# Attention and soft mixture of experts in one kernel: block sums as one product over four heads, the last values moved ahead of the last routing, shorter rings and three more weight buffers

## The chip, the cores and the metric

The kernel runs on one NeuronCore of a Trainium2 chip. The metric is the device time of one execution in microseconds (us), lower is better. The engines are TensorE (PE; its weight loads are listed apart as PEld), VectorE (DVE), ScalarE (ACT), GpSimd (POOL) and SyncE (SP), which issues the transfers between the chip's main memory and the on-chip buffers. Matrix products are written to PSUM banks, and DVE or ACT copies them out.

## The reference

Attention over 4 batches, 8 heads, 768 positions and 64 columns: each query sees the keys less than 16 positions away and 24 block keys. A block key is the largest value of each column over 32 positions; a block value is the mean over the same 32 positions. A soft mixture of 8 experts with 4 slots each follows on the 3072 x 512 result. All is float32.

```python
k_sum = k.reshape(B, H, nb, block, D).max(axis=3)
v_sum = v.reshape(B, H, nb, block, D).mean(axis=3)
scores_l = scale * np.matmul(q, k.transpose(0, 1, 3, 2))          # kept where |i - j| < 16
scores_s = scale * np.einsum('bhsd,bhnd->bhsn', q, k_sum) + np.log(block)
a = softmax(np.concatenate([scores_l_m, scores_s], axis=-1))
x = np.matmul(a, np.concatenate([v, v_sum], axis=2))              # to 3072 x 512
...
logits = x @ phi                                                  # 32 slots
d, c = softmax(logits, axis=0), softmax(logits, axis=1)
slot_input = d.T @ x
slot_out[e] = np.maximum(slot_input[e] @ w1[e], 0.0) @ w2[e]      # 8 experts, hidden 1024
return c @ slot_out
```

## The kernel before

**Steps.** The attention is cut into 24 steps (`NSTEP`): 8 half-batches `hb` of four heads, three steps each (`TPS`), and a step has 256 positions. The engines' work is written out by hand as three steps in flight. In loop turn `i` (L543) stand the scores of step `i` (L227, PE), their masked maxima (`soft_max`, L246, DVE) and exponentials; for the first head pair the exponential takes the maximum as a bias (L256, four ACT instructions), for the second POOL subtracts first (L262) and one ACT instruction follows (L258). The same turn transposes the weights of step `i-1` (`trans`, L268, PE; copied out by `evac`, L273, ACT) and multiplies those of step `i-2` with the values (`values`, L284, PE), which DVE divides by the sums (`norm`, L302 to L305). Each engine works through its own instructions in the order written; every wait is for another engine or a transfer.

**Block values.** `v_sum(hb)` (L313) forms the 24 block sums of four heads. A 0/1 matrix out of the constants picks the blocks; for each of 6 tiles of 128 positions, 2 halves `c` and 4 heads `g` there is one product of 32 x 64 outputs (L320), 48 in all. Half `c` has its own PSUM bank, and head `g` writes partitions 32g to 32g+31. Then four ACT copies (L331) and four DVE additions (L333) bring the 24 rows of each head to partitions 96 to 119 of `vsst`, and from there POOL copies them into the value tiles (`put_v`, L340), two copies a step. A table (`PLAN`, L41) says after which step each `V` begins (steps 0, 2, 5, 8, 11, 14, 17, 20): its products are issued at the end of that turn, its copies at the start of the next, ahead of that turn's `soft_max` (`held`, `flush`, L552).

**Routing.** The same table places the routing of the finished rows `x`: `X` transposes 128 rows (L351, copied by ACT, L354), `L` multiplies with `phi` (L364) and keeps a running maximum and its exponentials, `T` and `D` transpose these and add up `slot_input` (L396, L399, L407, L422). After the last step three more turns (24 to 26) hold the rest of the attention mixed with `X18` to `X23`, `L4`, `L5`, `T4` and `D4`; `T5`, `D5` and a few small products (`lanes`, `slots`) close it.

**Experts.** 64 weight pieces of 512 KB are read in order, the first 32 by the product `hps` (L647), the other 32 by `so` (L680), whose result is combined with the routing (`op`, L717) and written out. `LOADS` (L65) says how many pieces SP issues after each step. A piece goes to one of 39 places (`room`, L127): 17 buffers of its own (`NWA`), and tiles of the attention from the step on at which they are free.

**Rings.** The value tiles form a ring of 8 (`NV`), each loaded by two transfers (L160, L161) eight steps ahead of its use; the rows `x` a ring of 6 (`NX`); queries and keys have two buffers each, loaded at every third step (L151, L155).

Of the kernel before, what the change touches and what calls it, by code (L numbers as in the profile page):

```python
# [9 lines left out]
F32 = mybir.dt.float32  # L10
F32R = mybir.dt.float32r
AF = mybir.ActivationFunctionType
ALU = mybir.AluOpType
# [5 lines left out]
NB = S // 32  # L19
HB = 2 * B  # L20
TPS = 3
NSTEP = HB * TPS
NTT = 2 * TPS
# [14 lines left out]
NV, NQR, NX, NWA = 8, 2, 6, 17  # L38
# [21 lines left out]
    24: "X18 X19 | L4",  # L60
    25: "T4 ; X20 X21 | D4",
    26: "X22 X23 | L5",
}

LOADS = [0, 1, 1, 1, 1, 1, 1, 1, 1, 1, 1, 1, 1, 1, 1, 1, 1, 1, 1, 1, 5, 1, 1, 7, 1, 1, 2]  # L65
# [10 lines left out]
def attention_soft_moe(  # L76
# [13 lines left out]
    nc = tc.nc  # L90
# [24 lines left out]
    qs = [const.tile([128, TPS, 2, 256], F32, name=f"q{n}") for n in range(NQR)]  # L115
# [7 lines left out]
    qflat = [q.rearrange("p t r k -> p (t r k)")[:, 0:1024] for q in qs]  # L123
# [3 lines left out]
    room = [(t, 0) for t in was] + [(vflat[0], 18), (vflat[1], 19), (vflat[2], 20)]  # L127
    room += [(t, 20) for t in kflat[0] + [qflat[0]]] + [(vflat[3], 21), (vflat[4], 22), (vflat[5], 23)]
    room += [(t, 23) for t in kflat[1] + [qflat[1]] + xflat[0:2]] + [(vflat[6], 24), (vflat[7], 25)]
    room += [(t, 26) for t in xflat[2:4]] + [(t, 27) for t in xflat[4:]]  # L130
# [121 lines left out]
    def soft_exp(i, r):  # L252
        p, m = p_[i, r]
        if r == 0:
            for u in range(4):
                nc.scalar.activation(out=p[:, u, :], in_=p[:, u, :], func=AF.Exp, scale=-1.0, bias=m[:, u : u + 1])  # L256
        else:
            nc.scalar.activation(out=p, in_=p, func=AF.Exp)  # L258
# [12 lines left out]
    def evac(i, r):  # L271
        ptr = wk.tile([128, 4, 128], F32, name="ptr", bufs=4)
        nc.scalar.copy(out=ptr, in_=ptr_[i, r])  # L273
        ptr_[i, r] = ptr
# [38 lines left out]
    def v_sum(hb):  # L313
        pv = [post_bank(), post_bank()]
        for t in range(NTT):
            v = vs[(hb * TPS + t // 2) % NV]
            for c in range(2):
                for g in range(4):
                    o = C_IND + 22 - 2 * (2 * t + c)
                    nc.tensor.matmul(  # L320
                        pv[c][32 * g : 32 * g + 32, 0:64],
                        lhsT=cs[64 * c : 64 * c + 64, o : o + 32],
                        rhs=v[64 * c : 64 * c + 64, c, t % 2, g, 0:64],
                        start=(t == 0),
                        stop=(t == NTT - 1),
                        tile_position=(64 * c, 32 * g),
                    )
        yield
        st = vsst[96 : 96 + NB, hb % 2]
        for g in range(4):  # L330
            nc.scalar.copy(out=st[:, g, 0:64], in_=pv[0][32 * g : 32 * g + NB, 0:64])  # L331
        for g in range(4):
            nc.vector.tensor_tensor(  # L333
                out=st[:, g, 0:64], in0=pv[1][32 * g : 32 * g + NB, 0:64], in1=st[:, g, 0:64], op=ALU.add
            )
# [11 lines left out]
    def route_x(t):  # L347
        pv = post_bank()
        for c in range(4):
            x = xh[t // 2][:, t % 2, 128 * c : 128 * c + 128]  # L350
            nc.tensor.transpose(pv[:, 128 * c : 128 * c + 128], x, ident)  # L351
        yield
        xt = wk.tile([128, 4, 128], F32, name="xt", bufs=6)
        nc.scalar.copy(out=xt.rearrange("p c t -> p (c t)"), in_=pv)  # L354
        ps["xt", t] = xt


    def route_l(q):
# [17 lines left out]
        dt = wk.tile([128, 128], F32, name="dt", bufs=2)  # L376
# [17 lines left out]
    def route_t(q):  # L394
        pv = post_bank()
        nc.tensor.transpose(pv[:, 0:128], ps["dt", q], ident)  # L396
        yield
        dsb = wk.tile([128, 128], F32, name="dsb", bufs=2)
        nc.vector.tensor_copy(out=dsb, in_=pv[:, 0:128])  # L399
        ps["d", q] = dsb  # L400
# [96 lines left out]
    def flush(gs):  # L497
        for g in gs:
            while advance(g):
                pass  # L500
# [42 lines left out]
    for i in range(NSTEP + 3):  # L543
# [4 lines left out]
        if i < NSTEP:  # L548
            scores(i)
        if i == NSTEP + 1:  # L550
            tail.append(1)
        flush(held)  # L552
        if 0 <= a < NSTEP:
# [4 lines left out]
        if i < NSTEP:  # L558
            soft_max(i, 0)
            soft_exp(i, 0)  # L560
            soft_max(i, 1)
            soft_sub(i, 1)
# [5 lines left out]
        if 0 <= a < NSTEP:  # L568
            trans(a, 0)
            trans(a, 1)  # L570
            evac(a, 0)
            evac(a, 1)
        for group in front.split(";"):
            flush(begin(group))
        if i < NSTEP:
            soft_exp(i, 1)
        if 0 <= b < NSTEP:
            values(b)
            norm(b)
# [8 lines left out]
    flush(held)  # L588
    now[0] = NSTEP + 3
    gt = begin("T5")  # L590
    R = lanes()
# [10 lines left out]
    while len(wt) < NPRE:  # L602
        load_piece()
# [217 lines left out]
```

## Time and profile before

| | us |
|---|---|
| median of 3 runs | 222.17 |
| the 3 runs | 218.8, 222.17, 223.51 |
| the profiled execution, its own time | 219.1 |
| span of the profiled execution, first to last instruction | 217.3 |
| attention: first scores to the last product of `L5` | 9.0 to 154.7 |
| experts: first product of `hps` to the end of the span | 160.3 to 217.3 |

The profile is one execution of the program. Times in it count from its first instruction. "Busy" is the time in which an engine had an instruction running; the chain is the work that ended last, followed back from the end to what released each piece; "issue" is idle time of an engine for which the profile shows no releaser. A product of two float32 matrices stands in it as two MATMUL records, each with a LDWEIGHTS record; a transpose stands as one of each.

### The profile page before, as it was taken

The numbers are of one execution on the slowest core, as the hardware profiler recorded it, in microseconds if no ns is written. First come the engines' busy times: TensorE is split into PE (matmuls) and PEld (weight loads), VectorE is DVE, ScalarE is ACT, GpSimd is POOL, SyncE is SP. The second block draws the span as 40 slices with busy tenths as digits, with TensorE's granted clock in tenths as the row PEclk, the third lists the DMA queues.
The fourth block names the chain that finished last, engine by engine and source line by source line (L and its number), as shares of the span: only waits on it lengthen the run. The fifth ranks groups of instructions, "written<-read, shape, count | busy, mean of one in ns | idle before, by whom it ended". The sixth has DMA issues, their size and how long they took to land.

```text
span 217.3 us, 8616 instructions
## 1 busy us (share of the span) xinstructions
PE 178.3 (82%) x3473; PEld 132.1 (61%) x3473; DVE 128.4 (59%) x670; ACT 107.4 (49%) x277; POOL 76.6 (35%) x140
## 2 busy tenths in 40 slices
PE   7686986789879497986949998987789999999760
PEld 5464865677757485875739785874444555644450
DVE  1659597676869458686843866835345755033470
ACT  2057586757747465775545677773400222023360
POOL 8517659336528245642714554440010000000000
PEclk9888899999999889999975999999966999999997
DMA  6999999999967977894892539769998999998767
GB/s 221 329 376 290 376 270 250 369 242 284 358 191 246 336 200 217 306 263 135 269 296 76 149 119 310 272 210 360 420 323 269 391 418 417 419 415 354 305 276 303
DMA packets 19384, 63.19 MB, mean 291 GB/s; under 512 B 2320, under 2 KB 2320, under 8 KB 19344
## 3 DMA queue, kind: packets, MB, share of 16 engines
q1 hardware_dynamic: 19200, 62.28, 84.5%
q8 instruction: 27, 0.44, 0.9%
q10 hardware_dynamic: 144, 0.36, 0.5%
q14 instruction: 13, 0.11, 0.1%
HBM read 56.34 MB, written 6.29 MB: 288 GB/s over the span
## 4 chain that ended last, share of the span: by engine, by line
PE 53%; DVE 13%; ACT 10%; issue 8%; POOL 7%; DMA 6%; SPq 0%; POOLq 0%; ACTq 0%
PE hps L647 8%; PE so L680 7%; PE s L227 7%; PE pt L268 6%; PE o L284 6%; DVE p L246 5%; DMA kk<-kx 3%; PE op L717 3%; POOL p L262 3%; PE pp L351 3%; PE pp L407 3%; DMA q<-qx 3%; ACT xt L354 3%; ACT ptr L273 2%; PE pp L320 2%
## 5 line engine op out<-in xcount | busy, mean ns | idle before, releaser
L256 ACT ACTIVATE p<-p,m 128x128 f32<-128x128 f32 x96 | 30.7, 390 | 34.7 <-DVE m L246 34.7
L246 DVE CUSTOM_DVE_ANT_0 p<-s,cs 128x128 f32<-128x128 f32 x192 | 42.5, 286 | 8.8 <-PE s L227 8.3
L262 POOL TENSOR_TENSOR p<-m,p 128x512 f32<-128x512 f32 x24 | 24.9, 1038 | 61.4 <-DVE m L246 60.5
L227 PE MATMUL s<-kk,q 64*64 64x128 f32 x768 | 30.1, 282 | 12.1 <-issue 7.1
L227 PEld LDWEIGHTS s<-kk,q 64*64 64x64 f32 x768 | 23.1, 136 | 19.0 <-issue 13.6
L284 PE MATMUL o<-v,ptr 120*64 120x65 f32 (+1 forms) x768 | 29.8, 232 | 4.8 <-issue 4.8
L284 PEld LDWEIGHTS o<-v,ptr 120*64 120x64 f32 (+1 forms) x768 | 26.0, 144 | 9.5 <-issue 9.2
L340 POOL COPY v<-vsst 24x520 f32<-24x520 f32 x48 | 29.5, 615 | 5.8 <-DVE vsst L333 3.1
L268 PE MATMUL pt<-ident,p 128*128 128x128 f32 x192 | 29.9, 300 | 1.1 <-ACT p L258 0.9
L273 ACT COPY ptr<-pt 128x512 f32<-128x512 f32 x48 | 25.5, 577 | 3.1 <-PE pt L268 3.0
L268 PEld LDWEIGHTS pt<-ident,p 128*128 128x128 f32 x192 | 22.6, 151 | 6.7 <-issue 3.2
L180 DVE TENSOR_REDUCE ks<-kk 128x8 f32<-128x256 f32 x48 | 17.1, 412 | 6.7 <-DMA kk<-kx 6.6
L258 ACT ACTIVATE p<-p 128x512 f32<-128x512 f32 x24 | 15.3, 639 | 9.0 <-POOL p L262 9.0
L305 DVE TENSOR_TENSOR x<-o,z 128x256 f32<-128x256 f32 x48 | 18.1, 418 | 0.8
L246 DVE DVE_READ_ACCUMULATOR2_ANT m<- 128x1 f32 x192 | 15.9, 83 | 0.0
L302 DVE TENSOR_SCALAR z<-o 128x8 f32<-128x8 f32 x24 | 3.9, 164 | 19.2 <-PE o L284 18.9
L351 PE MATMUL pp<-ident,x 128*128 128x128 f32 x88 | 13.1, 296 | 0.0
L354 ACT COPY xt<-pp 128x512 f32<-128x512 f32 x22 | 12.2, 598 | 1.2 <-PE pp L351 1.2
L320 PE MATMUL pp<-v,cs 64*32 64x64 f32 x768 | 10.5, 235 | 2.3 <-issue 1.7
L351 PEld LDWEIGHTS pp<-ident,x 128*128 128x128 f32 x88 | 11.6, 156 | 0.0
L333 DVE TENSOR_TENSOR vsst<-pp,vsst 24x64 f32<-24x64 f32 x32 | 7.2, 224 | 7.3 <-ACT vsst L331 6.5
L647 PE MATMUL hps<-wa,W1ST 128*32 128x256 f32 x136 | 10.9, 468 | 0.5 <-DVE rz L479 0.5
(137 smaller groups left out, 217.0 us busy)
## 6 DMA issues: line engine op xcount, KB each, us to landing
wa<-w SPq DMA_DIRECT2D x34, 512.0 KB, 8.2
v<-w SPq DMA_DIRECT2D x12, 512.0 KB, 7.0
kk<-kx SPq DMA_DIRECT2D x7, 800.0 KB, 7.2
q<-qx SPq DMA_DIRECT2D x7, 768.0 KB, 9.7
v<-va SPq DMA_DIRECT2D x24, 195.0 KB, 6.6
v<-vb SPq DMA_DIRECT2D x24, 195.0 KB, 6.3
kk<-w SPq DMA_DIRECT2D x9, 512.0 KB, 7.4
x<-w SPq DMA_DIRECT2D x6, 512.0 KB, 7.7
```

Of the source, the lines that this page charges most:

```text
L227: nc.tensor.matmul(s[r][64 * c : 64 * c + 64, u, :].rearrange("p (a k) -> p a k", a=2), lhsT=qs[hb % NQR][64 * r : 64 * r + 64, tp, pr, o ...
L246: nc.vector.tensor_tensor_reduce(out=p[:, u, :], in0=s[:, u, :], in1=maskv[:, mk, :], scale=-0.125, scalar=-NEG, op0=ALU.add, op1=ALU.min, ...
L256: nc.scalar.activation(out=p[:, u, :], in_=p[:, u, :], func=AF.Exp, scale=-1.0, bias=m[:, u : u + 1])
L262: nc.gpsimd.tensor_tensor(out=p, in0=m.unsqueeze(2).broadcast_to([128, 4, 128]), in1=p, op=ALU.subtract)
L268: nc.tensor.transpose(pt[:, u, :], p[:, u, :], ident)
L273: nc.scalar.copy(out=ptr, in_=ptr_[i, r])
L284: nc.tensor.matmul(o[64 * c : 64 * c + 64, r, u, :], lhsT=ptr[0:K, u, 64 * c : 64 * c + 64], rhs=v[0:K, c, tt, 2 * pr + r, :], start=True, ...
L305: nc.vector.tensor_tensor(out=x[:, r], in0=o[:, r, :, 0:64].rearrange("p (t q) d -> p t q d", t=2), in1=z[:, r].rearrange("p (t q) -> p t ...
L340: eng.tensor_copy(out=vs[i % NV][n0 : n0 + NB, c].rearrange("n t h c -> n t (h c)"), in_=src.broadcast_to([NB, 2, 260]))
L351: nc.tensor.transpose(pv[:, 128 * c : 128 * c + 128], x, ident)
L354: nc.scalar.copy(out=xt.rearrange("p c t -> p (c t)"), in_=pv)
L647: nc.tensor.matmul(hps[32 * j : 32 * j + 32, :], lhsT=W1ST[:, c, 32 * e : 32 * e + 32], rhs=t[:, j, :], start=(k == 0), stop=(k == 31), ti ...
```

## The change

**Block sums.** `v_sum` takes all four heads of a tile and half in one product of 32 x 256 outputs: 12 products in place of 48. The four groups of 32 partitions now hold the sums of the tiles t with t % 4 = g, so partial sums. One ACT copy and one DVE addition over 128 x 256 (tile `vp`) join the two banks, one product with the constant `stk` (a matrix that adds rows 32 apart) folds the four groups, and one ACT copy brings 24 x 256 to `vsst`. The fold is issued after the next step's scores, and the last copy after that step's first four exponentials: `held` is advanced once after `scores`, and flushed after `soft_exp(i, 0)`.

PE, around the second block sum (V1, after step 2); first the kernel before, where `o` are the values' outputs, `pp` a bank of block sums and `s` scores:

```order
L284 MATMUL o<-v_93,ptr 64x65 x16
L320 MATMUL pp<-v_96,cs 32x64 x16
L320 MATMUL pp<-v_97,cs 32x64 x16
L320 MATMUL pp<-v_98,cs 32x64 x16
L227 MATMUL s_477<-kk_90,q_92 64x128 x2
```

and the changed kernel at the same place:

```order
L283 MATMUL o<-v_92,ptr 64x65 x16
L319 MATMUL pp<-v_95,cs 32x256 x4
L319 MATMUL pp<-v_96,cs 32x256 x4
L319 MATMUL pp<-v_97,cs 32x256 x4
L226 MATMUL s_400<-kk_90,q 64x128 x2
```

Each row of 16 products has become a row of 4 that are four times as wide. The fold stands behind the eight score rows that follow; PE in the changed kernel from the last of them on:

```order
L226 MATMUL s_401<-kk_90,q 64x128 x2
L332 MATMUL pp<-vp,cs 128x256
L267 MATMUL pt<-ident,p 128x128 x8
L283 MATMUL o<-v_93,ptr 64x65 x16
L226 MATMUL s_487<-kk_90,q 64x128 x2
```

The fold (L332) is ahead of the transposes, which had followed the scores directly. On ACT, the same place before, from the second exponential of step 2 on:

```order
L258 ACTIVATE p<-p 128x512
L331 COPY vsst<-pp 24x64 x4
L256 ACTIVATE p<-p,m 128x128 x4
L273 COPY ptr<-pt 128x512 x2
```

and in the changed kernel (here from the last block sum, V7, on):

```order
L257 ACTIVATE p<-p 128x512
L329 COPY vp<-pp 128x256
L255 ACTIVATE p<-p,m 128x128 x4
L334 COPY vsst<-pp 24x4x64
L272 COPY ptr<-pt 128x512 x2
```

Four small copies ahead of the exponentials became one wide copy ahead of them and one behind them.

**The end of the attention.** The turns 24 to 26 are written out apart from the loop. In the last step both head pairs take the exponential with the bias on ACT, and POOL subtracts nothing; one of step 22's two copies of transposed weights goes to DVE. PE, from the last two steps' weights to the end of `L5`, before (`tl` and `pp` are banks, `x_105`, `x_106` the last rows):

```order
L268 MATMUL pt<-ident,p 128x128 x8
L351 MATMUL pp<-ident,x_104 128x128 x8
L284 MATMUL o<-v_99,ptr 64x65 x16
L364 MATMUL pp<-xt,cs 32x128 x16
L396 MATMUL tl<-ident,dt 128x128
L351 MATMUL pp<-ident,x_105 128x128 x4
L351 MATMUL tl<-ident,x_105 128x128 x4
L284 MATMUL o<-v_100,ptr 64x65 x16
L407 MATMUL pp<-x_103,dsb 32x512 x2
L407 MATMUL pp<-x_104,dsb 32x512 x2
```

and in the changed kernel (`x_99`, `x_100` are the last rows there):

```order
L283 MATMUL o<-v_92,ptr 64x65 x16
L267 MATMUL pt<-ident,p 128x128 x4
L283 MATMUL o<-v_93,ptr 64x65 x16
L267 MATMUL pt<-ident,p 128x128 x4
L352 MATMUL pp<-ident,x_103 128x128 x8
L283 MATMUL o<-v_94,ptr 64x65 x16
L365 MATMUL pp<-xt,cs 32x128 x16
L352 MATMUL tl<-ident,x_99 128x128 x4
L352 MATMUL pp<-ident,x_99 128x128 x4
L352 MATMUL tl<-ident,x_100 128x128 x4
```

The last values (the third L283 row) stand ahead of `L4` (L365) and of the last four transposed row tiles; `T4` and `D4` now follow `L5`.

**Rings and buffers.** `NV` goes from 8 to 7, `NX` from 6 to 5, `NWA` from 17 to 20; the ring of transposed rows `xt` from 6 to 4, `dt` and `dsb` from 2 to 1. The two query buffers lie side by side, so that a third weight piece fits into them. With that `room` has 41 places, and `LOADS` is drawn up anew.

```diff
-NV, NQR, NX, NWA = 8, 2, 6, 17
+NV, NQR, NX, NWA = 7, 2, 5, 20
...
-    24: "X18 X19 | L4",
-    25: "T4 ; X20 X21 | D4",
-    26: "X22 X23 | L5",
...
     def v_sum(hb):
         pv = [post_bank(), post_bank()]
         for t in range(NTT):
             v = vs[(hb * TPS + t // 2) % NV]
+            g = t % 4
             for c in range(2):
-                for g in range(4):
...
+                nc.tensor.matmul(
+                    pv[c][32 * g : 32 * g + 32, 0:256],
+                    lhsT=cs[64 * c : 64 * c + 64, o : o + 32],
+                    rhs=v[64 * c : 64 * c + 64, c, t % 2, :, 0:64],
+                    start=(t < 4),
+                    stop=(t + 4 >= NTT),
+                    tile_position=(64 * c, 32 * g),
+                )
+        yield
+        vp = wk.tile([128, 256], F32, name="vp", bufs=1)
+        nc.scalar.copy(out=vp, in_=pv[0][:, 0:256])
+        nc.vector.tensor_tensor(out=vp, in0=pv[1][:, 0:256], in1=vp, op=ALU.add)
+        sp = post_bank()
+        nc.tensor.matmul(sp[:, 0:256], lhsT=stk, rhs=vp, start=True, stop=True)
+        yield
+        nc.scalar.copy(
+            out=vsst[96 : 96 + NB, hb % 2, :, 0:64], in_=sp[96 : 96 + NB, 0:256].rearrange("p (h d) -> p h d", h=4)
+        )
...
-    for i in range(NSTEP + 3):
+    for i in range(NSTEP):
...
+        scores(i)
+        held = [g for g in held if advance(g)]
+        soft_max(i, 0)
+        soft_exp(i, 0)
         flush(held)
...
+    j = NSTEP - 1
+    for c in range(2):
+        put_v(j, c, nc.gpsimd)
+    trans(j, 0)
+    values(j - 1)
+    loads(24, 1)
+    evac(j, 0)
+    trans(j, 1)
+    evac(j, 1)
+    gx = begin("X18 X19")
+    norm(j - 1)
+    values(j)
+    loads(25, 1)
+    flush(gx)
+    tail.append(1)
+    norm(j)
+    gl = begin("L4")
+    gx = begin("X20 X21")
+    flush(gl)
+    flush(gx)
+    gx = [route_x(22), route_x(23, True)]
...
+    gl = begin("L5")
+    flush(begin("T4"))
+    gd = begin("D4")
+    flush(gl)
     gt = begin("T5")
+    flush(gd)
```

More of the change, by code (lines that the diff above doesn't have):

```diff
@@ L114, in attention_soft_moe @@
     kk = [const.tile([128, KK_N], F32, name=f"kk{n}") for n in range(2)]
-    qs = [const.tile([128, TPS, 2, 256], F32, name=f"q{n}") for n in range(NQR)]
+    qb = const.tile([128, NQR, TPS, 2, 256], F32, name="q")
+    qs = [qb[:, n] for n in range(NQR)]
     vs = [const.tile([128, 2, 2, 4, 65], F32, name=f"v{n}") for n in range(NV)]
@@ L122, in attention_soft_moe @@
     vflat = [v.rearrange("p c t h d -> p (c t h d)")[:, 0:1024] for v in vs]
-    qflat = [q.rearrange("p t r k -> p (t r k)")[:, 0:1024] for q in qs]
+    qall = qb.rearrange("p n t r k -> p (n t r k)")
+    qflat = [qall[:, 1024 * n : 1024 * n + 1024] for n in range(3)]
     xflat = [x.rearrange("p t c -> p (t c)") for x in xs]
     kflat = [[k[:, 1024 * n : 1024 * n + 1024] for n in range(3)] for k in kk]
[L127 to L130, printed above, removed]
+    room = [(t, 0) for t in was] + [(vflat[3], 19), (vflat[4], 20)] + [(t, 20) for t in kflat[0] + [qflat[0]]]
+    room += [(vflat[5], 21), (xflat[2], 21), (vflat[6], 22), (vflat[0], 23)]
+    room += [(t, 23) for t in kflat[1] + qflat[1:]] + [(vflat[1], 24), (vflat[2], 25)]
+    room += [(t, 26) for t in xflat[3:]] + [(t, 27) for t in xflat[0:2]]
     NPRE = len(room)
@@ L269, in trans, with evac @@
         ptr_[i, r] = pt
-    def evac(i, r):
+    def evac(i, r, eng=None):
         ptr = wk.tile([128, 4, 128], F32, name="ptr", bufs=4)
-        nc.scalar.copy(out=ptr, in_=ptr_[i, r])
+        (eng or nc.scalar.copy)(out=ptr, in_=ptr_[i, r])
         ptr_[i, r] = ptr
@@ L316, in v_sum @@
             v = vs[(hb * TPS + t // 2) % NV]
+            g = t % 4
             for c in range(2):
-                for g in range(4):
[L319 to L327, printed above, removed]
-        yield
[L329 to L335, printed above, removed]
+                o = C_IND + 22 - 2 * (2 * t + c)
+                nc.tensor.matmul(
[6 more added lines that the diff above has]
+                )
+        yield
+        vp = wk.tile([128, 256], F32, name="vp", bufs=1)
[7 more added lines that the diff above has]
+        )
     def put_v(i, c, eng):
@@ L352, in route_x @@
         yield
-        xt = wk.tile([128, 4, 128], F32, name="xt", bufs=6)
-        nc.scalar.copy(out=xt.rearrange("p c t -> p (c t)"), in_=pv)
+        xt = wk.tile([128, 4, 128], F32, name="xt", bufs=4)
+        (nc.vector.tensor_copy if on_dve else nc.scalar.copy)(out=xt.rearrange("p c t -> p (c t)"), in_=pv)
         ps["xt", t] = xt
@@ L397, in route_t @@
         yield
-        dsb = wk.tile([128, 128], F32, name="dsb", bufs=2)
+        dsb = wk.tile([128, 128], F32, name="dsb", bufs=1)
         nc.vector.tensor_copy(out=dsb, in_=pv[:, 0:128])
@@ L557, in attention_soft_moe @@
             k_put(hb + 1, nc.gpsimd)
[L558 to L561, printed above, removed]
+        soft_max(i, 1)
+        if i < NSTEP - 1:
             soft_sub(i, 1)
@@ L571, in attention_soft_moe @@
             evac(a, 0)
[L572 to L577, printed above, removed]
+            evac(a, 1, nc.vector.tensor_copy if i == NSTEP - 1 else None)
+        flush(begin(front))
+        soft_exp(i, 1)
+        if b >= 0:
             values(b)
@@ L587, in attention_soft_moe, with loads @@
             load_piece()
-    flush(held)
-    now[0] = NSTEP + 3
+    def loads(step, n):
+        now[0] = step
+        for _ in range(n):
+            load_piece()
+    j = NSTEP - 1
[19 more added lines that the diff above has]
+    gx = [route_x(22), route_x(23, True)]
+    for g in gx:
+        advance(g)
+    flush(gx)
+    gl = begin("L5")
+    flush(begin("T4"))
+    gd = begin("D4")
+    flush(gl)
     gt = begin("T5")
+    flush(gd)
+    loads(26, 2)
     R = lanes()
@@ L601, in attention_soft_moe @@
     flush([slots()])
-    while len(wt) < NPRE:
-        load_piece()
+    loads(27, NPRE - len(wt))
     att.close()
```

16 lines of the change are left out of this document (6 added, 10 removed).

## The prediction

> **What bounds the kernel now.** I read the page's busy times first, then the waits, then PE's timeline where it waits for nothing named, then the windows with the granted clock.
>
> ```profile
> PE 178.3 (82%) x3473; PEld 132.1 (61%) x3473; DVE 128.4 (59%) x670; ACT 107.4 (49%) x277; POOL 76.6 (35%) x140
> q8 instruction: 27, 0.44, 0.9%
> PE s L227 <- issue: 7.1, 3, 3.2
> PE o L284 <- issue: 4.8, 3, 2.2
> PE pp L320 <- issue: 1.7, 1, 1.7
> ```
>
> PE is the busiest engine. The next rows are the key: a queue of its own brings instructions, 0.44 MB in 27 packets, so 16 KB each; and PE stands still seven times, 7.1 + 4.8 + 1.7 = 13.6 us, without a releaser. PE's timeline at two of these pauses (start, duration, work, and the idle time ahead):
>
> ```profile
> 31.73 0.92 PE L284 MATMUL o<-v,ptr 120*64 120x65 f32 x24 [0.85 <-issue]
> 32.58 1.10 PE L227 MATMUL s<-kk,q 64*64 64x128 f32 x32
> 33.62 1.09 PE L268 MATMUL pt<-ident,p 128*128 128x128 f32 x8
> 34.64 1.15 PE L284 MATMUL o<-v,ptr 120*64 120x65 f32 x32
> 35.72 0.45 PE L320 MATMUL pp<-v,cs 64*32 64x64 f32 x30
> 37.90 0.88 PE L320 MATMUL pp<-v,cs 64*32 64x64 f32 x66 [1.73 <-issue]
> 38.70 1.25 PE L227 MATMUL s<-kk,q 64*64 64x128 f32 x32
> 39.88 1.09 PE L268 MATMUL pt<-ident,p 128*128 128x128 f32 x8
> 40.81 1.04 PE L351 MATMUL pp<-ident,x 128*128 128x128 f32 x8
> 41.78 0.56 PE L284 MATMUL o<-v,ptr 120*64 120x65 f32 x11
> 44.09 0.85 PE L284 MATMUL o<-v,ptr 128*64 128x65 f32 x21 [1.74 <-issue]
> ```
>
> The pauses cut through the middle of groups that wait for nothing. Count what lies between them: 24 + 32 + 8 + 32 + 30 = 126 products up to the second, 66 + 32 + 8 + 8 + 11 = 125 up to the third. Each has a weight load, which makes 252 and 250, and a few semaphore instructions fill up to 256. The whole kernel agrees: 6946 products and loads over 27 packets are 257. So PE waits for its own next block of 256 instructions. A block under load takes 37.90 - 31.73 = 6.2 us to come, the next 44.09 - 37.90 = 6.2 us; blocks whose work is shorter end in a pause.
>
> The block sums use up blocks fastest: a `V` is 192 of these instructions in about 1.2 us. A plain step (scores, transposes, values) is 64 + 16 + 64 = 144 in 1.10 + 1.09 + 1.15, less the overlaps about 3.2 us.
>
> The clock is hurt by the same pauses (start:end, length, busy times with counts, granted clock, DMA share, GB/s):
>
> ```profile
> 26.00:72.00 46.00, 37.20 (x969) 31.04 (x968) 34.64 (x211) 31.30 (x82) 25.86 (x45) 1.00 0.95 281
> 72.00:80.00 8.00, 6.61 (x112) 6.00 (x111) 4.18 (x26) 4.54 (x12) 2.57 (x4) 0.79 0.83 261
> 111.00:119.00 8.00, 6.50 (x64) 5.72 (x68) 2.33 (x17) 3.84 (x9) 2.27 (x3) 0.57 0.55 153
> 160.30:167.00 6.70, 6.70 (x62) 2.63 (x66) 3.59 (x15) 0.62 (x2) 0.72 (x1) 0.54 0.91 290
> 167.00:210.00 43.00, 41.13 (x545) 23.77 (x538) 19.57 (x57) 12.19 (x25) 0.00 (x0) 1.00 0.92 368
> 112.50 0.69 PE L227 MATMUL s<-kk,q 64*64 64x128 f32 x4 [2.94 <-issue]
> 113.12 1.97 PE L268 MATMUL pt<-ident,p 128*128 128x128 f32 x8
> 114.89 1.91 PE L351 MATMUL pp<-ident,x 128*128 128x128 f32 x8
> 116.73 2.00 PE L284 MATMUL o<-v,ptr 120*64 120x65 f32 x32
> ```
>
> After the pause of 2.94 us the clock is at 0.57 and transposes, `X` and values take 1.97, 1.91 and 2.00 us in place of 1.09, 1.04 and 1.15. From 160 on PE is busy nearly throughout.
>
> **The change part by part.**
>
> *Fewer PE instructions.* A block sum goes from 48 products to 13; with two records and two loads each, from 192 instructions to 52, 1120 fewer over eight. Three plain steps and a `V` were 3 x 144 + 192 = 624 instructions in 3 x 3.2 + 1.2 = 10.8 us, 4.4 us for 256; now 484 in about 11.1 us, 5.9 us for 256. Against 6.2 us the lack falls from 1.8 to 0.3, and routing and small waits lengthen the blocks further. No block of the new order holds a whole old-style `V`, as the one before 112.50 did. I take 10.5 of the 13.6 us as saved; the ends are 13.6, and 4, if a faster PE packs the transfers closer and blocks come later.
>
> *The clock.* Lost now: (1 - 0.79) x 8 + (1 - 0.57) x 8 = 5.1 us of full clock. The pauses that open both windows should go; I take 3.5 us, ends 0 and 5.1. The window at 160.3 stays, since the small products ahead of it stay.
>
> *What the block sum costs PE.* Rows for it:
>
> ```profile
> 178.52 1.86 PE hps L647 x32
> 191.28 0.64 PE so L696 x4
> 129.28 0.63 ACT L258 ACTIVATE p<-p 128x512 f32<-128x512 f32 x1 [0.40 <-POOL p L262]
> 129.34 1.10 PE L227 MATMUL s<-kk,q 64*64 64x128 f32 x32
> 129.94 0.88 ACT L331 COPY vsst<-pp 24x64 f32<-24x64 f32 x4
> 130.17 0.99 DVE L333 TENSOR_TENSOR vsst<-pp,vsst 24x64 f32<-24x64 f32 x4 [0.83 <-ACT vsst L331]
> L354 ACT COPY xt<-pp 128x512 f32<-128x512 f32 x22 | 12.2, 598 | 1.2 <-PE pp L351 1.2
> L305 DVE TENSOR_TENSOR x<-o,z 128x256 f32<-128x256 f32 x48 | 18.1, 418 | 0.8
> ```
>
> The product has 24 passes of 256 columns. `hps` does 32 such passes, four at a time, in 1.86 us: that would be 1.4 us here, and 0.7 if all eight positions (two halves, four groups) run together. I take 1.05 us, against 1.17 before. The fold is two passes of 256 columns over the full array, as many columns as the four of 128 in 0.64 us: 0.45 to 0.6 us. New is a wait in PE's queue: the fold stands ahead of the transposes, and needs ACT's wide copy (behind the second exponential, which ends at 129.91; between the 0.2 us of a small copy and the 0.6 of a 128 x 512 one, so 0.4) and DVE's addition (0.42 as in L305). That is 130.8 with the hand-overs, and PE was through with the scores at 130.4: a wait of 0.4 us, with transposes, values and the next scores queued behind it. On DVE the addition is 0.42 where four took 0.99, so the maxima behind it come earlier. Per block sum 0.5 + 0.4 - 0.1 = 0.8 us, and the first is in the idle start: 7 x 0.8 = 5.5 us. Where PE waits for something else later anyway it is covered; ends 0 and 11 (product 1.4, wait 0.6). ACT's last copy, behind the exponentials, delays only `put_v`, which uses these sums a step later.
>
> *The end of the attention.*
>
> ```profile
> 138.64 1.10 PE L227 MATMUL s<-kk,q 64*64 64x128 f32 x32
> L256 ACT ACTIVATE p<-p,m 128x128 f32<-128x128 f32 x96 | 30.7, 390 | 34.7 <-DVE m L246 34.7
> 142.91 0.63 ACT L258 ACTIVATE p<-p 128x512 f32<-128x512 f32 x1 [0.46 <-POOL p L262]
> 153.62 1.07 PE tl L364 x26
> 160.29 1.08 PE hps L647 x8
> ```
>
> From the last scores (end 139.74) to `hps` it is 20.55 us. In the new order the second exponential is four ACT instructions of 30.7 / 96 = 0.32 us that wait for no subtraction of POOL's, with one copy fewer ahead of them: done about 143.4, where it was 143.54. From there I follow the order: transposes and their copy (0.45 + 0.6), the last values (1.15) with hand-overs to 146.2, the division on DVE (about 1.2) to 147.4. `L4` runs beside it; its softmax (DVE 0.5, ACT three small ones, 1.1) ends near 149.1, ACT's three copies of the last `X` (0.6 each; the fourth is DVE's) at 150.9, and `L5` (1.1) at 152.0 in place of 154.69. But `T4`, `D4` and the addition of `D4` on DVE now stand between `L5` and the last `dsb`, with 0.9 us at most. Net 2.7 - 0.9 = 1.8 us gained; ends 0 and 3.
>
> *Rings and buffers.* SP's queue loses one value load at the start and gains none elsewhere; the loads now come seven steps ahead.
>
> ```profile
> DVE ks L180 <- DMA kk<-kx: 6.6, 3, 3.9
> v<-va SPq DMA_DIRECT2D x24, 195.0 KB, 6.6
> ```
>
> A value load lands after 6.6 us, and the next block sum is two steps (some 10 us) off: covered; if two steps fell under 6.6 us, `V` would wait. Weights: in 167 to 210 PE is busy 41.13 of 43 us, so pieces are there in time; two more places and earlier loads are worth 0, and if that cover went, 1.3 us a piece (0.52 MB at some 400 GB/s). Shorter rings of `xt`, `dt` and `dsb`: the last reader is in each case ahead in PE's order, 0.
>
> *What is late next.* With PE earlier, DVE's maxima over the keys wait for their transfer (6.6 us in three waits today, some of them at the pauses), and `D` and `L` for ACT's copies. I add 2 us, ends 0 and 5.
>
> Sum against the profiled execution's own time: 219.1 - 10.5 - 3.5 + 5.5 - 1.8 + 2 = 210.8. That execution lies near the lowest of the three runs, 3.1 us under their median of 222.17. Part of that difference should be such pauses, which I expect to vanish, so I predict 211.
>
> [...]
>
> **The rivals.**
> 1. *The blocks come later too.* The same bytes in less time: each fetch stands behind denser transfers, and DVE waits for keys. Only 4 us of pauses are saved, 1.5 of clock, and 3 us of new waits come: 219.1 - 4 - 1.5 + 5.5 - 1.8 + 3 = 220; with the block sum half covered, 217. For it: DMA is at 0.95 in 26 to 72, where three pauses lie. Against it: the mean is 281 GB/s there and 368 in the experts' part.
> 2. *The fold holds PE (slower).* Its wait is not 0.4 but 3 us a time, because ACT's wide copy stands behind a late exponential and the transposes stand behind the fold. 7 x 2.6 = 18 more than my sum: 229. It decides the sign from 0.4 + 8.3 / 7 = 1.6 us of wait on. Against it: ACT comes free at 129.91, half a microsecond after the block sum.
> 3. *The change does not do it.* PE's pauses come from something that stays, and the clock with them: 219.1 + 5.5 - 1.8 = 222.8. For it: the profile names no releaser. Against it: the counts of 256.
>
> **How the numbers follow.** My forecast 0.68; rival 1 0.16, rival 3 0.10, rival 2 0.06. About 2% (4.4 us) is what a measurement of this kernel can tell from no change, so faster means under 217.7. The range takes 204 (all pauses and clock gone, block sums half covered: 219.1 - 13.6 - 5.1 + 3 - 1.8 + 2 = 203.6) to 218.5, with the better half of rival 1. Faster 0.79, the same 0.15, slower 0.06.
>
> **What would show it.** In the changed kernel's profile: PE's instruction packets 22 or 23 in place of 27; idle time under "issue" ahead of scores, values and block sums under 5 us in place of 13.6; clock at 1.00 through the middle of the attention; a block sum of 0.9 to 1.4 us, a fold of 0.5, and idle time ahead of the fold of 0.2 to 0.6 each; `hps` starting near 151 to 152. Wrong would be: pauses as long as before at the new block ends, idle time ahead of the fold over 1.5 us, or PE waiting for weight pieces after `hps` has begun.

## The result, and the profile after

| | before | after |
|---|---|---|
| median, us (4 runs each, on the same chip) | 220.49 | 204.22 |
| lowest and highest run | 216.41, 223.51 | 203.72, 204.59 |
| ratio after / before | | 0.938 (95%: 0.929 to 0.948) |
| the profiled execution, its own time | 219.1 | 204.04 |
| its span | 217.3 | 202.2 |
| end of the last scores | 139.74 | 127.12 |
| start of `hps` | 160.29 | 146.41 |
| `hps` to the end of the span | 57.0 | 55.8 |

The change made the kernel about 6% faster. The forecast was 211 us, "faster", in a range of 204 to 218.5: the direction is right, and the time lies only 0.2 us above the range's lower end. Of the 15.1 us by which the span fell, the sum had foreseen 8.3. (The ratio leaves disturbed runs out, so it is a little nearer to 1 than the quotient of the medians.)

The page of the changed kernel, with its busy times, the granted clock in 40 slices and PE's instruction queue:

```profile
PE 175.9 (87%) x2913; PEld 125.1 (62%) x2913; DVE 124.8 (62%) x648; ACT 104.8 (52%) x262; POOL 75.1 (37%) x138
...
PEclk9976999999999999999999999999979999999995
...
q8 instruction: 23, 0.38, 0.8%
```

560 records of PE and 560 weight loads are gone, and four of the 27 packets of instructions. The clock's row is to be held against the same row of the kernel before:

```profile
PEclk9888899999999889999975999999966999999997
```

Three dips were in it behind the start: at slices 14 and 15 (near 74 us), at 21 and 22 (112 to 119) and at 30 and 31 (160 to 167). In the changed kernel one is left, where `hps` begins (the last slices, in which both kernels end, apart). The waits of the changed kernel:

```profile
DVE ks L179 <- DMA kk<-kx: 12.4, 7, 3.9
DVE vp L330 <- ACT vp L329: 7.6, 7, 1.6
PE pp L332 <- DVE vp L330: 6.5, 6, 2.4
...
PE o L283 <- issue: 0.6, 1, 0.6
```

Of the seven pauses of PE without a releaser (13.6 us) one of 0.6 us is left. In their place PE waits ahead of the fold (L332): 2.4 us in the start, where nothing is lost, and 4.1 us in the other seven steps. DVE waits longer for the keys than before (12.4 us in place of 6.6).

The changed kernel by stretches (start:end, length, busy PE, PEld, DVE, ACT, POOL with counts, granted clock, DMA share, GB/s):

```profile
26.00:72.00 46.00, 42.10 (x821) 33.60 (x823) 35.78 (x221) 34.01 (x87) 27.86 (x48) 1.00 1.03 293
72.00:80.00 8.00, 6.95 (x159) 5.14 (x159) 7.00 (x35) 5.12 (x15) 3.82 (x8) 1.00 1.04 249
...
111.00:119.00 8.00, 7.85 (x166) 5.82 (x162) 5.84 (x36) 5.16 (x16) 5.13 (x10) 1.00 0.81 264
...
147.00:152.00 5.00, 5.00 (x66) 2.12 (x58) 3.22 (x14) 0.62 (x2) 0.14 (x1) 0.76 0.91 317
```

Between 26 and 72 us PE is busy for 42.1 us where it was 37.2, with fewer instructions; the two stretches at 0.79 and 0.57 are at 1.00. Around the second block sum (V1), all engines of the changed kernel, with the idle time ahead in brackets:

```profile
35.94 1.07 PE L319 MATMUL pp<-v,cs 64*32 64x256 f32 x24
...
36.10 0.79 POOL L202 COPY kk<-ks 128x288 f32<-128x288 f32 x2
...
36.86 1.03 POOL L261 TENSOR_TENSOR p<-m,p 128x512 f32<-128x512 f32 x1
...
36.94 1.20 PE L226 MATMUL s<-kk,q 64*64 64x128 f32 x32
...
37.92 0.63 ACT L257 ACTIVATE p<-p 128x512 f32<-128x512 f32 x1 [1.02 <-POOL p L261]
...
38.46 0.35 ACT L329 COPY vp<-pp 128x256 f32<-128x256 f32 x1
38.84 0.42 DVE L330 TENSOR_TENSOR vp<-pp,vp 128x256 f32<-128x256 f32 x1 [1.57 <-ACT vp L329]
...
39.32 0.70 PE L332 MATMUL pp<-vp,cs 128*128 128x256 f32 x2 [1.19 <-DVE vp L330]
...
39.86 1.04 PE L267 MATMUL pt<-ident,p 128*128 128x128 f32 x8
```

The block sum itself took 1.07 us, the fold 0.70, of which 0.54 are ahead of the next group. The wait of 1.19 us is a chain over four engines: POOL's copy for the next keys (36.10), POOL's subtraction behind it (36.86), ACT's second exponential (37.92), ACT's wide copy (38.46), DVE's addition (38.84), then the fold. The block sum was done at 37.0, and ACT came to its copy only at 38.46: the late link of the chain is POOL, not the copy. Counting PE's instructions in the traces, semaphore waits and weight loads included, sharpens what the prediction had read: all seven pauses of the kernel before stand at exactly 193 more than a multiple of 256 (numbers 961, 1217, 1473, 2241, 2753, 3777 and 4289, counted from 0). So not every wait in this kernel is for another engine or a transfer of its data: these 13.6 us stand at edges between PE's own instructions.

**Where the 15.1 us of span went.** I summed PE's records of both traces from 26 us to the end of the last scores. PE's idle time falls from 18.7 to 7.5 us: pauses at the edges of its instruction blocks 13.5 to 0.6, waits ahead of the fold 0 to 4.1, the rest 5.2 to 2.8. PE's busy time falls by 1.4 us: the seven folds add 3.8 (7 x 0.54), the block sums give back about 0.6, and the half-clock windows at 74 and 112 us, 5.1 us of full clock, are gone: 1.9 less by this count, 1.4 by the records. Together the last scores end 12.6 us earlier. From there to `hps` it is 19.3 us in place of 20.55 (1.3), and from `hps` on 55.8 in place of 57.0 (1.2; one half-clock window in place of two).

### The profile page after: what moved, and what is told of

It is laid out like the page before. It is cut to its first block, busy times and chain, and to the rows that moved or that the text cites. A ratio compares the mean times of both kernels' runs of the same rounds, so it can differ in the third digit from the quotient of the medians.

```text
span 202.2 us, 7435 instructions
## 1 busy us (share of the span) xinstructions
PE 175.9 (87%) x2913; PEld 125.1 (62%) x2913; DVE 124.8 (62%) x648; ACT 104.8 (52%) x262; POOL 75.1 (37%) x138
## 4 chain that ended last, share of the span: by engine, by line
PE 51%; DVE 16%; ACT 10%; POOL 9%; DMA 7%; issue 4%; SPq 0%; POOLq 0%; ACTq 0%
PE hps L678 8%; PE so L711 8%; DVE p L245 6%; PE o L283 6%; PE s L226 5%; POOL p L261 5%; PE pt L267 4%; DMA kk<-kx 4%; PE op L748 4%; PE pp L352 3%; DMA q<-qx 3%; PE pp L365 2%; PE pp L408 2%; POOL v L341 2%; ACT p L255 2%
## 5 line engine op out<-in xcount | busy, mean ns | idle before, releaser
L255 ACT ACTIVATE p<-p,m 128x128 f32<-128x128 f32 x100 | 32.0, 391 | 27.8 <-DVE m L245 27.7
L226 PE MATMUL s<-kk,q 64*64 64x128 f32 x768 | 28.1, 281 | 2.1 <-DVE kk L202 2.1
L283 PE MATMUL o<-v,ptr 120*64 120x65 f32 (+1 forms) x768 | 27.9, 225 | 1.5 <-DVE x L304 0.9
L226 PEld LDWEIGHTS s<-kk,q 64*64 64x64 f32 x768 | 22.0, 136 | 11.1 <-issue 3.4
L267 PE MATMUL pt<-ident,p 128*128 128x128 f32 x192 | 27.7, 285 | 0.6 <-ACT p L257 0.5
L283 PEld LDWEIGHTS o<-v,ptr 120*64 120x64 f32 (+1 forms) x768 | 24.5, 137 | 5.7 <-issue 5.0
L179 DVE TENSOR_REDUCE ks<-kk 128x8 f32<-128x256 f32 x48 | 17.1, 412 | 12.4 <-DMA kk<-kx 12.4
L332 PE MATMUL pp<-vp,cs 128*128 128x256 f32 x16 | 6.1, 467 | 6.6 <-DVE vp L330 6.5
L352 PEld LDWEIGHTS pp<-ident,x 128*128 128x128 f32 x88 | 9.8, 141 | 1.9 <-ACT vsst L334 1.5
L319 PE MATMUL pp<-v,cs 64*32 64x256 f32 x192 | 10.3, 415 | 0.2 <-ACT xt L355 0.2
L748 PE MATMUL op<-sls,cT 128*128 128x256 f32 x48 | 9.1, 311 | 1.0 <-DVE sls L735 0.9
```

Of the source, the lines that this page charges most:

```text
L226: nc.tensor.matmul(s[r][64 * c : 64 * c + 64, u, :].rearrange("p (a k) -> p a k", a=2), lhsT=qs[hb % NQR][64 * r : 64 * r + 64, tp, pr, o ...
L267: nc.tensor.transpose(pt[:, u, :], p[:, u, :], ident)
L283: nc.tensor.matmul(o[64 * c : 64 * c + 64, r, u, :], lhsT=ptr[0:K, u, 64 * c : 64 * c + 64], rhs=v[0:K, c, tt, 2 * pr + r, :], start=True, ...
L748: nc.tensor.matmul(op[-1][:, 256 * g : 256 * g + 256], lhsT=cT[:, t, :], rhs=sl, start=True, stop=True)
```

## The experiments

In the table, "pauses" are the idle times of PE at the edges of its blocks of 256 instructions, summed over the records of each profiled execution; ratios are to the kernel before on the same chip. They did not all run on the same chip (the kernel before has medians of 220.1 to 222.3 us on them), so ratios are compared across all of them, and times and spans of different chips only roughly.

| kernel | ratio (95%) | span | pauses | last scores end | `hps` starts |
|---|---|---|---|---|---|
| before | | 217.3 | 13.5 | 139.7 | 160.3 |
| changed | 0.938 (0.929 to 0.948) | 202.2 | 0.6 | 127.1 | 146.4 |
| e1 changed, old block sums | 0.994 (0.989 to 1.000) | 216.3 | 12.9 | 140.9 | 160.2 |
| e2 before, new block sums | 0.948 (0.939 to 0.956) | 204.1 | 0.0 | 127.8 | 148.5 |
| e3 before, 128 instructions more at the start | one run, 220.46 us | 218.7 | 17.2 | 141.1 | 162.0 |
| e4 changed, 140 instructions more per block sum | 0.999 (0.993 to 1.005) | 215.9 | 9.2 | 140.8 | 160.0 |
| e5 changed, fold behind the transposes | 0.952 (0.944 to 0.960) | 210.0 | 0.0 | 134.8 | 154.1 |
| e6 changed, three key buffers | 0.939 (0.931 to 0.948) | 207.5 | 3.0 | 130.7 | 150.9 |
| e8 changed, old rings and buffers | 0.929 (0.921 to 0.937) | 203.6 | 0.4 | 128.1 | 147.4 |
| changed, once more | 0.934 (0.926 to 0.943) | 203.4 | 0.1 | 128.2 | 147.5 |
| e9 changed, wide copy early | 0.928 (0.919 to 0.937) | 202.5 | 0.8 | 125.2 | 145.3 |
| e10 as e9, idle PE filled | 0.927 (0.920 to 0.934) | 200.6 | 1.1 | 125.9 | 145.2 |
| e11 changed, 128 instructions more at the start | 0.939 (0.930 to 0.948) | 205.6 | 2.6 | 130.4 | 149.7 |

### The change in two halves: e1 and e2

The first kernel is the changed one with the 48 small products, four copies and four additions of before:

```diff
             for c in range(2):
-                nc.tensor.matmul(
-                    pv[c][32 * g : 32 * g + 32, 0:256],
+                for g in range(4):
+                    nc.tensor.matmul(
+                        pv[c][32 * g : 32 * g + 32, 0:64],
...
```

> The changed kernel with the block sums as they were (48 products of 64 columns, four copies, four additions); the new end, rings and buffers stay. If the gain comes from fewer PE instructions: 27 instruction packets again, over 10 us of PE idle under issue, 214 to 219 us. If the end of the attention and the buffers bring it: under 208 us.

The second is the kernel before with the new block sums and the order that goes with them, and nothing else (`dt` and `dsb` with one buffer, to make room for `vp`):

```diff
+        held = [g for g in held if advance(g)]
+        if i < NSTEP:
+            soft_max(i, 0)
+            soft_exp(i, 0)
         flush(held)
...
-            soft_max(i, 0)
-            soft_exp(i, 0)
```

> The kernel before with the new block sums alone (dt and dsb have one buffer each, to make room for vp); end, rings and weight places as before. If the gain comes from fewer PE instructions: 22 or 23 packets, under 3 us of PE idle under issue, 205 to 209 us. If the end and the buffers bring it: over 214 us.

Both came out as the theory had it (medians of 218.0 and 207.0 us). With the old block sums 27 packets and the pauses are back; the waits of that kernel:

```profile
PE s L226 <- issue: 6.9, 3, 3.8
...
PE o L283 <- issue: 4.6, 3, 2.2
```

With the new block sums alone there are 23 packets, and the clock is full through the middle of the attention; the kernel's page:

```profile
PEclk9998899999999999999999999999969999999995
...
q8 instruction: 23, 0.38, 0.8%
```

The half with the block sums has the ratio 0.948 alone, the other half 0.994, and their product, 0.942, is within the interval of the whole. The new end of the attention is the other half: from the last scores to `hps` it is 19.2 us in e1 against 20.55 before, and 19.3 in the changed kernel against 20.6 in e2. It is 1.3 us in both pairs.

### Is it the number of PE's instructions? e3 and e4

The pauses could also follow certain steps, and the gain could come from the denser products themselves. The first kernel moves the blocks' edges: the kernel before with 32 small products (64 records, 64 loads) ahead of everything, whose outputs nobody reads.

```diff
+    for _ in range(32):
+        nc.tensor.matmul(wm[0:32, 256:320], lhsT=acc[:, 0:32], rhs=acc[:, 0:64], start=True, stop=True)
```

> The kernel before with 32 more small products (128 instructions) in PE's idle start, results unused. If PE's pauses are waits for its next block of 256 instructions, each stands 128 instructions earlier in the program: the one that cut a block sum after 30 of 96 products moves to the end of the transposes two groups ahead of it, and the one after 28 of 32 scores moves into the values or the block sum ahead of it; 7 or so pauses in all, 215 to 225 us. If those products wait for something of their own, the pauses stay where they were.

The pauses moved by 128 instructions. PE's timeline of that kernel at two places:

```profile
39.14 1.16 PE L320 MATMUL pp<-v,cs 64*32 64x64 f32 x94
42.51 0.30 PE L320 MATMUL pp<-v,cs 64*32 64x64 f32 x2 [2.21 <-issue]
...
110.18 0.82 PE L320 MATMUL pp<-v,cs 64*32 64x64 f32 x61
111.40 0.54 PE L320 MATMUL pp<-v,cs 64*32 64x64 f32 x35 [0.40 <-issue]
...
119.40 1.33 PE L227 MATMUL s<-kk,q 64*64 64x128 f32 x23 [2.88 <-issue]
```

The pause that had stood 11 products into the values behind V1 now stands 94 records into V1 itself; from there to the old place it is 2 + 32 + 8 + 8 + 11 = 61 records with as many loads, 122 instructions. The one of 2.94 us behind 28 of 32 scores has become 0.40 us at 61 of 96 records of the block sum ahead of them, and the next edge, in the scores of the step after, pauses for 2.88. So a pause belongs to an edge between blocks, not to a step: all ten pauses of this kernel stand at the same instruction numbers, 193 more than a multiple of 256. In sum they grew to 17.2 us, 2.9 of them in the first 26 us, and the time stayed (220.46 us, one run). How long the pause is goes with the place of the edge in a step (2.94 us at that one, 0.40 and 2.88 here).

The second gives the changed kernel its old number of instructions back: 35 products of 64 columns behind each block sum, 3473 records on PE as before, with outputs that nobody reads.

```diff
+        for n in range(35):
+            c, g = n // 4 % 2, n % 4
+            nc.tensor.matmul(
+                pv[c][32 * g : 32 * g + 32, 256:320],
+                lhsT=cs[64 * c : 64 * c + 64, C_IND : C_IND + 32],
+                rhs=v[64 * c : 64 * c + 64, c, 1, g, 0:64],
...
```

> The changed kernel with 35 more small products (140 instructions, as many as the change removed) behind each block sum's products, results unused. They take PE about 0.85 us a time by the old products' rate, 6 to 7 us in all: 211 us if only their work counts. If the number of instructions counts, pauses of 8 us or more and half-clock windows come on top: 215 to 222 us.

The whole gain was gone: 0.999. Its waits, and two of its stretches:

```profile
PE s L226 <- issue: 4.7, 2, 3.1
...
PE pt L267 <- issue: 2.8, 1, 2.8
...
PE o L283 <- issue: 1.0, 2, 0.5
```

```profile
72.00:80.00 8.00, 6.98 (x107) 6.22 (x107) 3.50 (x23) 4.42 (x10) 2.27 (x3) 0.79 0.62 175
...
111.00:119.00 8.00, 5.17 (x59) 4.44 (x50) 3.26 (x20) 3.98 (x10) 2.33 (x4) 0.79 0.78 235
```

Block sum and padding held PE for 1.8 us where the block sum alone took 1.07, so 7 x 0.75 = 5.3 us of the 13.7 us of span are the products' own time (the first block sum costs nothing: its fold starts at 16.54 us in place of 16.57). The rest are the pauses (9.2 in place of 0.6) and the clock in these two stretches (2 x 0.21 x 8 = 3.4 us), less the 4.1 us that PE had waited ahead of the folds, now covered: 5.3 + 8.6 + 3.4 - 4.1 = 13.2. Instructions that do nothing bring back the pauses (9.2 us) and, with them, the dips of the clock (0.79 in both stretches).

### Rings, buffers and keys: e8 and e6

```diff
-NV, NQR, NX, NWA = 7, 2, 5, 20
+NV, NQR, NX, NWA = 8, 2, 6, 17
...
-        xt = wk.tile([128, 4, 128], F32, name="xt", bufs=4)
+        xt = wk.tile([128, 4, 128], F32, name="xt", bufs=6)
```

(with `room` and `LOADS` of before.)

> The changed kernel with the rings and weight places as before (8 value tiles, 6 row tiles, 17 weight buffers, 6 of xt; 39 places and the former counts of loads). If rings and buffers are worth nothing, as forecast: 203 to 205.5 us. If the weight buffers carry part of the gain: over 207 us; if the shorter rings cost: under 202 us.

The ratio is 0.929 where the changed kernel had 0.934 and 0.938, the intervals overlap, and from `hps` on it took 203.6 - 147.4 = 56.2 us against 55.8. In time it is 206.68 us, outside the ranges given, on a chip where the kernel before takes 222.33. Shorter rings and three more weight buffers are worth nothing that can be measured here.

DVE's waits for keys had doubled, so the next kernel has a third key buffer, loaded two steps earlier, at the price of the three weight buffers:

```diff
-NV, NQR, NX, NWA = 7, 2, 5, 20
+NV, NQR, NX, NWA, NK = 7, 2, 5, 17, 3
...
-            k = kk[hb % 2][:, K0:EA0]
+            k = kk[hb % NK][:, K0:EA0]
...
```

> The changed kernel with a third key buffer, loaded two steps earlier, and 17 weight buffers of its own in place of 20 (the third key buffer gives three places from step 18 on). DVE's waits for keys (12.4 us in seven waits) should go below 3 us. If PE sets the end, these waits are covered: 203 to 205 us. If they are on the path: 199 to 201 us.

The waits for keys fell to 7.4 us, two of them, both in the first 16 us, and the kernel was no faster: 0.939, with 208.71 us where e8 took 206.68 on the same chip. Neither forecast held. Its profile shows two pauses of 1.0 and 1.8 us that the changed kernel did not have, and a mean granted clock of 0.956 against 0.962; `hps` starts 4.4 us later. So pauses can still come by small shifts. That the longer waits for keys are covered fits this, but with the new pauses in it the run does not show it cleanly.

### The wait ahead of the fold: e5 and e9

Two ways to take the fold out of PE's way. In the first it is issued behind the transposes, and the last copy behind ACT's copies of the transposed weights:

```diff
-        flush(held)
+        if i == 1:
+            flush(held)
...
+            held = [g for g in held if advance(g)]
...
-        flush(held)
```

> The changed kernel with the fold behind the next step's transposes on PE and the last copy behind the copies of the transposed weights (the first block sum as it was). If PE's waits ahead of the fold (4.1 us over the second to the eighth block sum in the changed kernel's profile) are on the path that sets the end: 200 to 201 us. If other waits take their place: 203.5 to 205 us.

Both theory and rival failed: it is slower than the changed kernel, with a span of 210.0. The timeline of PE and ACT at the same block sum:

```profile
40.19 0.60 PE L334 MATMUL pp<-vp,cs 128*128 128x256 f32 x2
40.62 0.60 PE L354 MATMUL pp<-ident,x 128*128 128x128 f32 x4
41.13 1.04 ACT L272 COPY ptr<-pt 128x512 f32<-128x512 f32 x2
42.20 0.36 ACT L336 COPY vsst<-pp 24x256 f32<-24x256 f32 x1
42.59 1.31 ACT L357 COPY xt<-pp 128x512 f32<-128x512 f32 x2
42.62 0.66 PE L354 MATMUL pp<-ident,x 128*128 128x128 f32 x4 [1.40 <-ACT vsst L336]
```

The fold no longer waits (40.19, right behind the transposes). But the second half of `X` needs the bank that the fold wrote, and that is free only when ACT has copied it out (42.20), now behind the two larger copies. PE waits 1.40 us there, and 8.2 us in six such waits; the 4.1 us ahead of the fold became twice as much behind it. I had reckoned with the fold's inputs and not with the bank that it holds.

In the second the wide copy and the addition go ahead of the second exponential, so that they do not wait for POOL:

```diff
+        yield
         vp = wk.tile([128, 256], F32, name="vp", bufs=1)
...
-        soft_exp(i, 1)
+        if "V" not in back:
+            soft_exp(i, 1)
...
+        if "V" in back:
+            held = [g for g in held if advance(g)]
+            soft_exp(i, 1)
```

> The changed kernel with ACT's wide copy and DVE's addition ahead of that step's second exponential; the fold stays where it is. ACT sits idle for 1.0 us ahead of that exponential in the steps in which the fold waits longest, so by this theory the waits ahead of the fold go to under 1 us in all and the time to 200.5 to 202 us. If the fold waits for something else than that copy: 203.5 to 205 us.

It gave a ratio of 0.916 (0.904 to 0.929), from two runs; the median of all four, 204.96 us, is not the 200.5 to 202 us expected, though its profile has no wait ahead of the seven folds any more. To tell it from the changed kernel both were run on one chip, the same edit as e9:

> The changed kernel once more, as the measure for the next three on the same chip. Expected 203.5 to 206 us where the kernel before takes 219 to 222, the ratio 0.93 to 0.945, and at most 1.5 us of idle time of PE without a releaser inside the attention.

> The changed kernel with ACT's wide copy and DVE's addition moved ahead of the second exponential, so that the fold does not wait behind it. Theory: the 4.1 us that PE waits ahead of the seven folds inside the attention lie on the path; with the copy early PE waits there under 2 us and the kernel is 1 to 3 us faster than the changed one on this chip. Rival: the steps end with a wait of PE for DVE's keys or for its instructions in any case, so what is taken off the fold comes back there; then the last scores end within 0.7 us of where they do in the changed kernel, and the time is within 1 us of it.

The waits ahead of the seven folds are gone, and the last scores end 3.0 us earlier than in the changed kernel on that chip; of the 4.5 us of waits there, 1.9 came back, most of it as waits of `X` and `L`. In the time it is 204.62 against 205.63 us (medians of six runs, 202.2 to 205.9 and 204.0 to 206.8): 1 us, at the lower edge of what the theory asked for, and the intervals of the two ratios overlap. So the waits are on the path, as the place of the last scores shows; how much of them reaches the end is not settled. In e9's profile the clock took part of it back, which is the next experiment's subject.

### The clock at the start of the experts: e10

In e9 PE ran at half clock from 142.8 to 149.6, twice as long as the changed kernel at this place. In this kernel seven unused products of 128 columns break up PE's idle time between `L5` and `hps`:

```diff
+    fill(3)
     flush(gt)
...
+    fill(2)
     flush(gd)
     flush([R])
     flush([slots()])
+    fill(2)
```

> As the kernel with the early copy, with seven unused products of 128 columns (they go to a bank that nobody reads) in PE's idle time between the last L and hps. Theory: the half-clock window that opens at the end of the attention (146 to 149 us in the changed kernel, 3.4 us) follows the idle time of PE ahead of it; with that idle time broken up PE keeps its clock, hps starts no later, and the experts' part is 1.5 us shorter, so 1 to 2 us less than the kernel with the early copy. Rival: the window comes in any case or later, or PE's idle time was not its cause: the same time within 0.7 us, or slower by what the seven products take of the path (up to 1 us).

The stretch from 144 to 150 us and the clock's row, first of e9, then of e10:

```profile
144.00:150.00 6.00, 5.46 (x46) 2.40 (x49) 2.86 (x13) 0.50 (x2) 1.06 (x1) 0.53 0.87 272
```

```profile
PEclk9976999999999999999999999999579999999995
```

```profile
144.00:150.00 6.00, 5.98 (x80) 3.44 (x80) 3.58 (x16) 0.62 (x2) 1.06 (x1) 1.00 0.98 362
```

```profile
PEclk9967999999999999999999999999999999999995
```

In the same six microseconds PE handled 64 records of `hps` in place of 40 (four of the 80 records belong to the unused products). `hps` starts no later (145.2 against 145.3), and from there to the end it is 55.4 us in place of 57.2. That is the mechanism as expected, in one profile each; the granted clock over the whole span, which every run has, agrees: in the mean of six runs each 0.970 in e10, 0.958 in e9 and 0.955 in the changed kernel. The median, 203.82 us, is the lowest of the three on that chip. It is 0.8 us under e9's, between what theory (1 to 2 us) and rival (within 0.7) had said, so the time does not decide between them. Against the changed kernel's 205.63 it is 1.8 us; the six runs lie between 202.4 and 204.6 against 204.0 and 206.8, and the intervals of the ratios overlap, so a gain is likely and not shown.

### Was the changed kernel lucky? e11

```diff
+    for _ in range(32):
+        nc.tensor.matmul(wm[0:32, 256:320], lhsT=acc[:, 0:32], rhs=acc[:, 0:64], start=True, stop=True)
```

(the edit of e3, here on the changed kernel.)

> The changed kernel with the 32 small unused products (64 instructions with their loads, 128 records counted as in the shifted kernel before) at the start, so that every block of 256 instructions of PE begins at another place in the steps. Theory: with about six us of work in a block the places hardly matter; pauses without a releaser of 0 to 3 us in all, and the time within 2.5 us of the changed kernel's, 204 to 207 us. Rival: the changed kernel has been lucky in where its blocks end; then pauses of 5 us and more come back and with them a half-clock window, 210 us or more.

As the theory had it: 206.58 us against 205.63, with two pauses, of 1.6 and 0.9 us. With these edges the changed kernel loses about 1 us in the medians, and 2.2 us of span in the profiled executions, not 13. One shift by 128 instructions was tried, no other.

## Why the prediction was right, and where it was off

The mechanism was the one that the prediction named, and the sizes were not: the gain in span was nearly twice the sum. PE waited for its own instructions, the change removed a sixth of them, and the pauses and the dips of the clock went with them. e1, e2, e3 and e4 show this from four sides. The sizes, term by term, against the profiled execution:

| term of the sum | predicted | measured | from |
|---|---|---|---|
| pauses of PE | -10.5 | -12.9 | edges of blocks, 13.5 to 0.6 |
| clock | -3.5 | -5.1, and about -1.2 in the experts | the stretches; `hps` to the end |
| block sums on PE | +5.5 | +7.3 | 4.1 waits + 3.8 folds - 0.6 |
| end of the attention | -1.8 | -1.3 | last scores to `hps` |
| rings and buffers | 0 | 0 | e8 |
| what is late next | +2 | -2.4 | PE's other waits, 5.2 to 2.8 |
| sum | -8.3 | -15.6 | the span says -15.1 |

That the range still held it is partly luck. Its lower end was worked out with the block sums half covered, at 3 us, and with all pauses and dips gone. The block sums cost 7.3; what made up for that were the waits of the last row, and the clock in the experts, for which neither the sum nor the range had a gain.

*Pauses.* I had taken 6.2 us for a block to come and 5.9 us of work in one, which left a lack of 0.3 us. From the trace's packets the blocks of the changed kernel are entered 5.5 to 8.8 us apart in the attention, and only one came late. Four more came just in time: there, as at a pause, PE went on 1.3 to 1.5 us after the packet had landed, 5.5 to 6.6 us after the edge before. So the 6.2 us for a block was about right, and most of the other blocks held more work than the 5.9 us. That the blocks would come later in a denser stream (rival 1) did not happen, though transfers were as dense: DMA share 1.03 in place of 0.95 between 26 and 72 us. (Four pauses lay in that stretch, not three as that rival says.)

*Clock.* I kept 1.6 us back for the chance that windows open for another reason. The dips at both places in the attention followed pauses, and both went; e2 (pauses 0.0, no dips there) and e4 (pauses 9.2 us, clock 0.79 in both stretches) show the same. One term was missing: of the two windows in a row at 160 us only one came in the changed kernel. Why the second did not is not shown. It may not be the change's doing: the padded e4 has one window at this place (PE at half rate from 160.0 to 163.3), e9 and e6 have two (142.8 to 149.6 and 148.4 to 154.6).

*Block sums.* (The prediction's 7 x 0.8 is 5.6, not 5.5.) The product was forecast at 1.05 us and took 1.07 in most steps; the fold at 0.45 to 0.6 and takes 0.54. The wait was forecast at 0.4 a time. It was 1.2 in three steps, 0 to 0.3 in the others, 0.6 in the mean. The row that I took it from (ACT free at 129.9, half a microsecond behind the block sum) was of one step; in the three steps in which POOL's copy of the new keys runs right ahead of its subtraction, as in the lines above, the exponential ahead of the wide copy is late. In the other four POOL stood idle for 0.9 to 1.6 us before it subtracted. That is rival 2's mechanism, at well under half of the 1.6 us from which it would have decided.

*What is late next.* This is the term that was most off, in sign too. I added 2 us for waits on keys and on ACT's copies. The waits on keys did double, and e6 gives no sign that they are on the path. PE's other waits in the attention became shorter, most of them waits of `D` and `L` for their inputs; in the changed kernel's second profile they are about 3.5 us in place of 2.8, so part of the 2.4 us is the difference between one execution and the next. That pauses had pulled engines out of step in the kernel before, and that with the pauses gone these inputs are ready more often, is argued, not shown by a run of its own.

*End of the attention.* `L5` was to end at 152.0, counted in the old kernel's time with the last scores unmoved, that is 12.3 us behind the last scores; it ended at 139.7, 12.6 behind them. The rest, to `hps`, was as expected. The term was 0.5 us too good.

*Rival 3*, that the change does not do it, was priced at 222.8 and is out.

## What to carry to other kernels

Where PE stands idle without a releaser, count its instructions between the pauses: if the count is one number each time or a multiple of it (256 here), the number of instructions is the price (140 more per block sum took the whole gain in e4), and fewer, wider products paid here although their own time grew: 1.07 us and 0.54 for the fold in place of 1.17 a block sum, at a ratio of 0.948 in e2. Price such a pause with the half-clock stretch that can follow it: each window of 3.4 us cost 1.7 us here, on top of pauses of about 3 us. When a step is moved out of the way, follow the buffer it holds as well as the inputs it needs: moving the fold behind the transposes removed 4.1 us of waits ahead of it and put 8.2 us behind it.

## What the runs showed of the hardware that was not expected

- **How late a block comes.** From the packets of PE's instruction queue: in the kernel before PE entered a block at 31.73, the packet of the next one ran from 35.34 to 36.55, and PE went on at 37.90. Ahead of the seven pauses PE went on 1.3 to 1.7 us after the packet had landed. In the attention of the changed kernel the next packet began 0.4 to 4.7 us after PE had entered a block. That fits one block ahead of PE and no more in these two traces, and most of the 6.2 us (3.6 at this block) is the time until the packet starts.
- **The clock's dips have one length.** In the traces of both kernels, apart from the window in which they end, PE is at half clock (0.50) for 3.4 us at a time, once or twice in a row; behind the first 26 us these are, before, 74.33 to 77.74, 111.88 to 118.70 and 159.66 to 166.49, and in the changed kernel 145.99 to 149.41. In the kernel before two of the three places followed a pause of about 3 us (3.2 us from 70.2 on, 2.94 from 109.6 on). The other pauses of that kernel, up to 2.19 us, had no window behind them. But in e3 one came behind a pause of 2.24 us (the 32 scores behind it took 1.99 us in place of 1.10) and none behind one of 2.21 (there they took 1.22, behind a block sum, where they take 1.25 at full clock before): no length decides it alone. At the end of the attention one came behind a run of waits of 0.4 to 0.7 us, 2.0 us together (changed kernel, 140.0 to 146.4), and with unused products in them the clock stayed at 1.00 (e10).
- **The start varies.** In the first 26 us the dips of the clock lie in other slices from one profile to the next in kernels whose start is the same: of the rows above, e9's begins with 9976 and e10's with 9967.
